# Table checks of a Fourier-plus-experts kernel: four W checks and the row check cut into steps, six compares moved to the score part, no dots in the last block but one

## The chip, the cores and the metric

The kernel runs on one core of a Trainium2 chip. A core has a matrix engine (TensorE, PE in the profile; its weight loads are PEld), a vector engine (VectorE, DVE), a scalar engine (ScalarE, ACT), a general engine (GpSimd, POOL), and SyncE (SP), which here issues most of the DMA transfers. Every engine takes its own instructions in the order written; engines wait for each other through semaphores. The metric is the device time of one execution in microseconds (us). For the kernel before it is 1112.83 us, the median of three runs (1112.5 to 1113.57).

## The reference

With `xn` the layer norm of `x` (2048 tokens, 512 features), the output is `x + A + B`.

```python
# A: real part of a two-dimensional Fourier transform, by given DFT matrices
a = einsum("bsd,ed->bse", xn, dft_hid_re);  b = einsum("bsd,ed->bse", xn, dft_hid_im)
A = einsum("ts,bse->bte", dft_seq_re, a) - einsum("ts,bse->bte", dft_seq_im, b)
# B: 32 heads; each token picks 2 of 64x64 experts per head
q = einsum("nd,dhc->nhc", xn, w_q)
s1 = einsum("nhd,ed->nhe", q[..., :128], k1);  s2 = einsum("nhd,ed->nhe", q[..., 128:], k2)
# top 2 of s1 and of s2, then the top 2 of the 4 sums: top_e (expert), g (softmax weight)
act = gelu(einsum("nd,nhkd->nhk", xn, u[top_e]))
B = einsum("nhk,nhk,nhkd->nd", g, act, v[top_e])
```

The DFT matrices are inputs like any other. The kernel uses their symmetries (it folds rows and columns together and multiplies a quarter of the matrix), so it must also check that the matrices it was given have these symmetries; if one had not, a general path at the end of the program would be taken. The tables are checked by reading their mirrored parts side by side, subtracting (or adding) them, and summing absolute values.

## The kernel before

**Three parts follow each other.** A first part (up to about 70 us) normalises `x` and does the Fourier transform with folded matrices. The score part (72 to 442 us) runs 8 groups of heads times 16 token tiles: 12 matmuls (L799) give a tile's scores, ACT copies them out of PSUM (L804), DVE takes the best of each 64 (L807, L811), and POOL and DVE turn them into expert numbers and gates. Part B (from about 457 us) works on blocks of 128 tokens, 14 of them, numbered 0 to 13. The last two tiles of tokens take another way: their experts' rows are fetched one by one.

**One block of part B.** `u_part(b)` (L959) multiplies the block by all of `u` in 8 steps, called cg here, of 48 matmuls; after each step ACT applies the gelu (L962). The gates are put into a dense matrix by `g_mm(b, tg)` (L996), four times per block: DVE builds two one-hot tables `L` (L983, twice) and `R` (L991, L994), and PE multiplies them into a pair of PSUM banks called `g`. `w_part(b, tg)` then makes weights: DVE multiplies `act` by `g` in place (L1007), ACT rounds to 16 bit (L1012), DVE takes the remainder (L1015). `v_part(b)` (L1024) multiplies by `v` in 8 steps of 12 matmuls, and `finish(b)` (L1039) adds the result to `y` and stores it. The program runs `v_part(b)`, then `u_part(b + 2)`, with `g_mm` and `w_part` of the blocks between them at fixed steps. There are two pairs of `g` banks, so a `g_mm` can start only when the L1015 of the `g_mm` two before it is done. A block has four L1015; the last stands on DVE shortly before the block's `finish`. Blocks 12 and 13 have no `u_part` after them; block 12 is the last but one. The stretch of a block on DVE is counted here from the `finish` of the block before it to its own.

**What runs beside it.** Three streams fill DVE, ACT and POOL. (1) Checks: `compare(n)` for n in 0 to 63 loads 512 KB of the sequence matrices into a buffer of the ring `w` (three buffers, `WB`), DVE subtracts the mirrored parts (L755, L761; other lines where a tile holds row 0), ACT sums absolute values (L781, L783). `compare_w(n)`, n = 64 to 67, does the same with the hidden matrices W, and `compare_r(64)` with rows 0. (2) `fit(n)` has ACT measure largest values of the scaled weights, also in a `w` buffer. (3) The dots of the last two token tiles: POOL fetches a row (L1050), DVE multiplies and sums it (L1066), ACT scales it (L1076 to L1079), POOL adds it (L1084).

**What sets the order.** Each step of `v_part` or `u_part` calls `paced`, which takes the next entries of a list so that the list ends on time, in turn for the fits and for the checks (`units`), and `pick`, which takes dots. `after(k, f)` puts `f` off by k steps, and `hold` ties its instructions behind the step's last matmul in the order of the program; this order is fixed when the program is built, and adds no wait. The compares in `EARLY` are done in the score part instead, at the steps in `at_k`: there POOL subtracts in place of DVE, and the ring `cx` with three buffers is used. `verdict()` sums all checks up in the last block.

Of the kernel before, what the change touches and what calls it, by code (L numbers as in the profile page):

```python
# [15 lines left out]
AF = mybir.ActivationFunctionType  # L16
# [20 lines left out]
def tile_fnet_peer(ctx, tc, x, ca, cb, c5, wt, wf, wr, wq, kt, ut, vn, uv, out):  # L37
# [55 lines left out]
    EARLY = [*range(8, 24), *range(40, 52)]  # L93
# [462 lines left out]
    def part_b(safe, stS, stP, stE, xt, u_sb, cmp_p):  # L556
# [299 lines left out]
        at_k = [7, 10, *(16 * j + i for j in range(1, 7) for i in (0, 4, 7, 9) if (j, i) != (2, 0)), 112, 122, 125]  # L856
# [252 lines left out]
        def compare_r(n):  # L1109
# [14 lines left out]
            def work():  # L1124
                for ri, odd, e in cls:
                    sgn = (((1, 1, 1), (-1, 1, -1)), ((-1, -1, 1), (1, -1, -1)))[ri][odd]
                    f = (-1 if ri else 1) * sgn[1] * sgn[2]
                    m = ALU.add if ri else ALU.subtract
                    nc.vector.tensor_tensor(tv[e, 1], tv[e, 1], tv[e, 0], op=ALU.subtract if sgn[0] > 0 else ALU.add)
                    nc.vector.tensor_tensor(tv[e, 3], tv[e, 3], tv[e, 2], op=ALU.subtract if f > 0 else ALU.add)  # L1130
                    nc.vector.tensor_tensor(t[e, 0::2, 2:4], t[e, 0::2, 2:4], t[e, 0::2, 0:2], op=m)
                    if odd and ri:
                        nc.vector.tensor_copy(t[e, 2, 0:2], t[e, 0, 0:2])
                    elif odd == ri:
                        nc.vector.memset(t[e, 2, 0:2], 0.0)
                after(2, lambda: nc.scalar.activation(tf[:, P:], tf[:, P:], AF.Abs, accum_out=chk[:, n:n + 1]))

            after(2, work)

        def compare_w(n):  # L1140
# [7 lines left out]
            if half:  # L1148
# [4 lines left out]
            nc.vector.tensor_reduce(asum[:, n:n + 1], v[0], axis=AX.X, op=ALU.add, apply_absolute_value=True)  # L1153
            nc.vector.tensor_tensor(v[1][:, even], v[1][:, even], v[0][:, even], op=op)
            nc.vector.tensor_tensor(v[1][:, odd], v[1][:, odd], v[0][:, odd], op=po)
            nc.vector.tensor_tensor(v[3][0:1], v[3][0:1], v[2][0:1], op=op)
            nc.vector.scalar_tensor_tensor(v[3][:, even], v[0][:, even], not0, v[3][:, even],  # L1157
                                           op0=ALU.mult, op1=ALU.subtract)
            nc.vector.scalar_tensor_tensor(v[3][:, odd], v[0][:, odd], not0, v[3][:, odd],  # L1159
                                           op0=ALU.mult, op1=ALU.add)  # L1160

            r = v[2][0:1]
            a, m = (slice(0, P, 2), slice(P, 256, 2)) if ri else (slice(1, P - half, 2), slice(P + 1, 256 - half, 2))
            nc.vector.tensor_tensor(r[:, m], r[:, m], r[:, a], op=op)  # L1164
            nc.vector.memset(r[:, 1 - ri:P:2], 0.0)  # L1165
            if half and not ri:
                nc.vector.memset(r[:, 255:256], 0.0)
            nc.vector.scalar_tensor_tensor(v[2], v[0], not0, v[2], op0=ALU.mult, op1=op)  # L1168
            if ri:
                nc.scalar.activation(v[0][0:1, 0:P], v[0][0:1, 0:P], AF.Abs, accum_out=chk[0:1, 69 + half:70 + half])  # L1170
            c = P - half
            nc.vector.tensor_tensor(v[0][:, P:P + c], v[0][:, P:P + c], v[0][:, 0:c], op=op)  # L1172
            if half and not ri:
                nc.vector.memset(v[0][:, 255:256], 0.0)
# [318 lines left out]
```

## Time and profile before

| What | us |
|---|---|
| median of three runs | 1112.83 |
| the profiled execution | 1110.31 |
| its span, first to last instruction | 1108.5 |
| PE busy | 1070.5 (97%) |
| DVE busy | 963.9 (87%) |
| ACT busy | 717.3 (65%) |
| POOL busy | 595.4 (54%) |

The profiled execution lasted 1.8 us longer than its span, which leaves out what lies around the first and the last instruction. A row of the timeline has the start and the duration in us, the engine, the line, the operation, the output and inputs by the program's names, the shape, how many were merged (x), and in brackets how long the engine sat idle before it and what ended that. A row of the view by windows has, for one stretch, the busy time of each engine with its number of instructions, then the granted clock of the matrix engine (1.00 is full speed), the share of the DMA engines, and GB/s.

### The profile page before, as it was taken

What the parts mean: (1) busy time and instruction counts of PE and PEld (TensorE: products, weight loads), DVE (VectorE), ACT (ScalarE), POOL (GpSimd) and SP (SyncE); (2) the same over time, 40 slices, a digit from 0 to 9 for tenths busy, and PEclk for the clock granted to TensorE, in tenths of its full rate; (3) what the DMA queues carried; (4) which work ended last, traced back from release to release, by engine and by line L of the source; (5) the groups of instructions that cost most, each with busy time, mean ns of one, the idle gap of its engine ahead of it and who ended that gap; (6) DMA issues with size and microseconds to landing.
All of it is one profiled execution on the core that took longest, in us unless ns stands there. A gap on an engine that the chain in (4) does not pass through costs nothing. (4 is left out here: it accounts for less than half of the span.)

```text
span 1108.5 us, 28483 instructions
## 1 busy us (share of the span) xinstructions
PE 1070.5 (97%) x11070; PEld 696.6 (63%) x11070; DVE 963.9 (87%) x2748; ACT 717.3 (65%) x1326; POOL 595.4 (54%) x553
## 2 busy tenths in 40 slices
PE   5899999999999999999989999999999999999987
PEld 4355555454544544987675967858667696776933
DVE  6879897979999999987999798999998889998971
ACT  3566657778788767533756766668666776767650
POOL 0013537588797846211646575665575656556431
PEclk9799999999999999999999999999999999999999
DMA  8248153435445331463568667766876667666511
GB/s 326 84 168 288 39 210 99 174 130 208 152 153 197 110 123 65 152 212 92 183 189 248 193 206 244 223 220 191 242 232 214 209 204 252 222 200 200 166 29 51
DMA packets 84936, 196.78 MB, mean 178 GB/s; under 512 B 10770, under 2 KB 27559, under 8 KB 84792
## 3 DMA queue, kind: packets, MB, share of 16 engines
q1 hardware_dynamic: 63898, 123.55, 33.0%
q0 software_dynamic: 20736, 71.31, 21.7%
q8 instruction: 88, 1.44, 0.5%
q14 instruction: 56, 0.46, 0.1%
q10 hardware_dynamic: 158, 0.01, 0.0%
HBM read 177.74 MB, written 17.10 MB: 176 GB/s over the span
## 5 line engine op out<-in xcount | busy, mean ns | idle before, releaser
L799 PE MATMUL s<-m,xq 128*128 128x512 f16 x1536 | 338.9, 379 | 0.0
L959 PE MATMUL z<-xb,u 128*128 128x128 f16 x5376 | 306.4, 220 | 0.0
L959 PEld LDWEIGHTS <-u 128*128 128x128 f16 x5376 | 302.1, 98 | 0.0
L1024 PE MATMUL v<-v,act 128*128 128x512 f16 x1344 | 300.2, 382 | 1.6 <-DVE act L1015 1.6
L1084 POOL TENSOR_TENSOR ov<-ov,ga 128x512 f32<-128x512 f32 x128 | 176.9, 1382 | 206.9 <-ACT ga L1079 173.4
L799 PEld LDWEIGHTS <-xq 128*128 128x128 f16 x1536 | 148.3, 98 | 171.3 <-issue 0.2
L1024 PEld LDWEIGHTS <-act 128*128 128x128 f16 x1344 | 129.6, 98 | 153.2 <-issue 4.5
L983 DVE TENSOR_TENSOR L<-io_lam,cmp 128x2048 f16<-128x2048 f16 x112 | 154.7, 1405 | 31.2 <-PE g L996 31.1
L1050 POOL DMA_INDIRECT ga<-in_uv_dram,eix x128 | 153.4, 1198 | 48.1 <-POOL ov L1084 36.9
L807 DVE MAX8 vals<-ss 128x8 f32<-128x64 f32 x1024 | 152.5, 216 | 14.0 <-ACT ss L804 14.0
L962 ACT ACTIVATE act<-z,scl 128x512 f32<-128x512 f32 x112 | 76.1, 681 | 93.6 <-PE z L959 92.9
L811 DVE FIND_INDEX8 idx<-vals,ss 128x8 uint16<-128x256 f32 x256 | 107.1, 419 | 0.0
L804 ACT ACTIVATE ss<-s,wsc 128x512 f32<-128x512 f32 x112 | 75.5, 680 | 43.1 <-PE s L799 33.8
L1079 ACT ACTIVATE ga<-ga,za 128x512 f32<-128x512 f32 x128 | 92.3, 722 | 10.2 <-ACT za L1077 0.4
L781 ACT ACTIVATE cx<-cx 128x896 f32<-128x896 f32 x64 | 60.6, 947 | 48.7 <-DVE cx L761 36.3
L1066 DVE SCALAR_TENSOR_TENSOR ga<-ga,px 128x512 f32<-128x512 f32 x128 | 85.7, 676 | 0.2
L1012 ACT ACTIVATE act<-g 128x1024 f16<-128x1024 f32 x56 | 73.2, 1308 | 18.2 <-DVE g L1007 18.2
L1007 DVE SCALAR_TENSOR_TENSOR g<-act,scl,g 128x1024 f32<-128x1024 f32 x56 | 71.6, 1279 | 10.7 <-ACT act L962 6.6
L1015 DVE TENSOR_TENSOR act<-g,act 128x1024 f16<-128x1024 f32 x56 | 72.7, 1298 | 6.6 <-ACT act L1012 6.5
L169 POOL TENSOR_TENSOR wq<-wq,wh 128x1024 f16<-128x1024 f32 x26 | 55.5, 2136 | 24.2 <-ACT wq L166 23.7
L996 PE MATMUL g<-R,L 128*128 128x32 f16 x1792 | 53.8, 176 | 13.0 <-DVE act L1015 12.5
L996 PEld LDWEIGHTS <-L 128*128 128x128 f16 x1792 | 51.6, 96 | 21.7 <-DVE act L1015 8.7
(281 smaller groups left out, 1298.4 us busy)
## 6 DMA issues: line engine op xcount, KB each, us to landing
cx<-in_cb_dram SPq DMA_DIRECT2D x50, 448.0 KB
wq<-in_wq_dram SPq DMA_DIRECT2D x32, 512.0 KB
fit<-in_wq_dram SPq DMA_DIRECT2D x28, 512.0 KB
uv<-in_ut_dram SPq DMA_DIRECT2D x16, 512.0 KB
uv<-in_vn_dram SPq DMA_DIRECT2D x16, 512.0 KB
cx<-in_cb_dram SPq DMA_DIRECT2D x28, 224.0 KB
xq<-in_x_dram SPq DMA_DIRECT2D x8, 512.0 KB
xt_d<-xq SPq DMA_DIRECT2D x16, 256.0 KB
```

The costliest lines, as they stand in the source:

```text
L799: mm = nc.tensor.matmul(ps, xt[i][:, l, kd, :], m[:, r, kd, :], start=(n == 0), stop=(n == 3 * KD - 1))
L807: nc.vector.max(vals[:, i, w, :, h], s[:, g, :])
L811: nc.vector.max_index(idx[:, i, w].rearrange("p k h -> p (k h)"), vals[:, i, w, 0:2].rearrange("p k h -> p (k h)"), s[:, w * HC:g + 1, :]. ...
L959: mm = nc.tensor.matmul(p[:, cc * P:(cc + 1) * P], ug[:, l, c % 2, kd, :], xb[:, r, kd, :], start=(n == 0), stop=(n == 3 * KD - 1))
L962: GL[mm.ins.name] = nc.scalar.activation(act[:, cg * 4:cg * 4 + 4, :].rearrange("p c n -> p (c n)"), p, AF.Gelu_apprx_tanh, scale=zsc)
L983: nc.vector.tensor_tensor(L.rearrange("p t (l two) -> p t l two", two=2), io_lam.rearrange("p (l two) -> p l two", two=2).unsqueeze(1).to_ ...
L996: i = nc.tensor.matmul(p[:, hf, t * NC:(t + 1) * NC], L[:, t, :], R[:, hf * 16 + t, :], start=True, stop=True)
L1024: mm = nc.tensor.matmul(pv, w16[:, c, :, l], vg[:, r, c % 2, :], start=(c == 0 and k == 0), stop=(c == NC - 1 and k == 2))
L1050: nc.gpsimd.indirect_dma_start(out=t, out_offset=None, in_=uv, in_offset=bass.IndirectOffsetOnAxis(ap=eix[:, n].rearrange("p k h -> p (k h ...
L1066: nc.vector.scalar_tensor_tensor(t, t, 1.0, T["x"], op0=ALU.mult, op1=ALU.mult, accum_out=T["z", n][:, s:s + 1])
L1079: nc.scalar.activation(t, t, AF.Copy, scale=z)
L1084: T["a"] = nc.gpsimd.tensor_tensor(o, o, t, op=ALU.add)
```

## The change

Four things change. `EARLY` has 34 compares instead of 28 (38, 39 and 52 to 55 are added), so six more run in the score part (steps 18, 22, 34, 44, 46, 115 and 118 are new in `at_k`, step 23 is gone), and 30 instead of 36 are left for part B. The four `compare_w` go from the end of the list of checks to places 3, 9, 15 and 21 of it, and `compare_r` from place 2 to place 6; by the pacing, the work of the W checks on DVE then falls in the stretches of blocks 2, 4, 6 and 8 and that of the rows in the stretch of block 3, where before W fell in those of blocks 11 and 12 and the rows in that of block 1. `compare_w` no longer does its ten to twelve DVE instructions at once but in four pieces, one each at 2, 3, 4 and 5 steps behind the load, and the sum on ACT at 7; `compare_r` does its four classes at steps 3 to 6 and the sum at 8. The dots picked in block 12 are left out there and picked in block 13. From L857 on, lines of the changed kernel are one higher, and more from L1125 on.

```diff
-    EARLY = [*range(8, 24), *range(40, 52)]
+    EARLY = [*range(8, 24), *range(38, 56)]
...
-        at_k = [7, 10, *(16 * j + i for j in range(1, 7) for i in (0, 4, 7, 9) if (j, i) != (2, 0)), 112, 122, 125]
+        at_k = [7, 10, 16, 18, 20, 22, 25, 34, 36, 39, 41, 44, 46,
+                *(16 * j + i for j in range(3, 7) for i in (0, 4, 7, 9)), 112, 115, 118, 122, 125]
...
         def compare_r(n):
...
-            def work():
-                for ri, odd, e in cls:
...
-                after(2, lambda: nc.scalar.activation(tf[:, P:], tf[:, P:], AF.Abs, accum_out=chk[:, n:n + 1]))
-
-            after(2, work)
+            for k, c in enumerate(cls):
+                after(3 + k, lambda c=c: work(*c))
+            after(8, lambda: nc.scalar.activation(tf[:, P:], tf[:, P:], AF.Abs, accum_out=chk[:, n:n + 1]))
...
         def compare_w(n):
...
-            after(2, lambda: nc.scalar.activation(f, f, AF.Abs, accum_out=chk[:, n + 1:n + 2]))
+            for k, part in enumerate((first, second, third, last)):
+                after(2 + k, part)
+            after(7, lambda: nc.scalar.activation(f, f, AF.Abs, accum_out=chk[:, n + 1:n + 2]))
...
-        units.insert(2, lambda: compare_r(64))
+        for n in range(4):
+            units.insert(3 + 6 * n, units.pop())
+        units.insert(6, lambda: compare_r(64))
...
                 if b and b + 2 != NB:
                     pick(mm, 2 if b + 1 == NB else 1)
-                elif b:
-                    pick(mm, cg % 2)
```

The order of DVE at three places shows what this moves. A row has the line, the operation, the outputs and inputs with buffer numbers, and the shape; `cx_r` is the tile of the row check, `cx` that of a compare or a W check, `ga` a dot, `g` a `w_part`'s product, `act` its remainder.

**The row check.** Before, on DVE in block 1, ahead of the block's last `act`:

```order
L1130 TENSOR_TENSOR cx_r<-cx_r 4x256
L1066 SCALAR_TENSOR_TENSOR ga_9_7478,za_7117<-ga_9_7478,px_7116 128x512
L1131 TENSOR_TENSOR cx_r<-cx_r 4x2x128
L1129 TENSOR_TENSOR cx_r<-cx_r 3x256
L1130 TENSOR_TENSOR cx_r<-cx_r 3x256
L1007 SCALAR_TENSOR_TENSOR g_2_7709<-act_6973,scl,g_2_7709 128x32x32
L1131 TENSOR_TENSOR cx_r<-cx_r 3x2x128
L1129 TENSOR_TENSOR cx_r<-cx_r 4x256
L1130 TENSOR_TENSOR cx_r<-cx_r 4x256
L1015 TENSOR_TENSOR act_6973<-g_1_7583,act_6973 128x32x32
```

After, on DVE in block 3, ahead of the second `act`:

```order
L1129 TENSOR_TENSOR cx_r<-cx_r 3x256
L1130 TENSOR_TENSOR cx_r<-cx_r 3x256
L1067 SCALAR_TENSOR_TENSOR ga_25_8643,za_7165<-ga_25_8643,px_7164 128x512
L1131 TENSOR_TENSOR cx_r<-cx_r 3x2x128
L1135 MEMSET cx_r 3x128
L1129 TENSOR_TENSOR cx_r<-cx_r 4x256
L1130 TENSOR_TENSOR cx_r<-cx_r 4x256
L1067 SCALAR_TENSOR_TENSOR ga_26_8716,za_7165<-ga_26_8716,px_7164 128x512
L1016 TENSOR_TENSOR act_7810<-g_3_8673,act_7810 128x32x32
```

Five of the twelve subtractions now stand ahead of this `act`; the others follow, ahead of the third one.

**The last block but one.** Before, on DVE in block 12, between the first `g` of block 13 and its `act`, with a W check and a dot between them:

```order
L1007 SCALAR_TENSOR_TENSOR g_0_16064<-act_15714,scl,g_0_16064 128x32x32
L1157 SCALAR_TENSOR_TENSOR cx_16377<-cx_16377,not_87 128x128
L1159 SCALAR_TENSOR_TENSOR cx_16377<-cx_16377,not_87 128x128
L1164 TENSOR_TENSOR cx_16377<-cx_16377 1x64
L1007 SCALAR_TENSOR_TENSOR g_1_16340<-act_15714,scl,g_1_16340 128x32x32
L1165 MEMSET cx_16377 1x64
L983 TENSOR_TENSOR L_5792<-io_lam,cmp_15718 128x2048
L1168 SCALAR_TENSOR_TENSOR cx_16377<-cx_16377,not_87 128x256
L1066 SCALAR_TENSOR_TENSOR ga_61_16011,za_11802<-ga_61_16011,px_11801 128x512
L983 TENSOR_TENSOR L_5793<-io_lam,cmp_15718 128x2048
L1172 TENSOR_TENSOR cx_16377<-cx_16377 128x127
L1015 TENSOR_TENSOR act_15714<-g_0_16064,act_15714 128x32x32
```

After, at the same place:

```order
L1008 SCALAR_TENSOR_TENSOR g_0_16078<-act_15737,scl,g_0_16078 128x32x32
L1008 SCALAR_TENSOR_TENSOR g_1_16344<-act_15737,scl,g_1_16344 128x32x32
L984 TENSOR_TENSOR L_5839<-io_lam,cmp_15741 128x2048
L992 TENSOR_TENSOR R_5841<-io_c,cmp_15741 128x1024
L755 TENSOR_TENSOR cx_16381<-cx_16381 128x256
L755 TENSOR_TENSOR cx_16381<-cx_16381 128x512
L995 TENSOR_TENSOR R_5841<-R_5841,cmp_15741 128x1024
L1016 TENSOR_TENSOR act_15737<-g_0_16078,act_15737 128x32x32
```

Six W instructions and a dot are gone from between the two; one `L` has moved ahead, and `R` and a compare have come in. In the order of PE, the `g_mm` that waits for this `act` stands 36 matmuls of `v_part` behind the one before it, where it stood 39 behind it.

**The end of a block.** Before, on DVE at the end of block 9, up to the block's last `act`:

```order
L1007 SCALAR_TENSOR_TENSOR g_2_14070<-act_13340,scl,g_2_14070 128x32x32
L991 TENSOR_TENSOR R_5794<-io_c,cmp_14134 128x1024
L994 TENSOR_TENSOR R_5794<-R_5794,cmp_14134 128x1024
L1066 SCALAR_TENSOR_TENSOR ga_32_13994,za_11802<-ga_32_13994,px_11801 128x512
L1015 TENSOR_TENSOR act_13340<-g_1_13947,act_13340 128x32x32
```

After, at the same place:

```order
L1008 SCALAR_TENSOR_TENSOR g_2_14893<-act_14167,scl,g_2_14893 128x32x32
L1067 SCALAR_TENSOR_TENSOR ga_42_14670,za_11838<-ga_42_14670,px_11837 128x512
L992 TENSOR_TENSOR R_5840<-io_c,cmp_14960 128x1024
L995 TENSOR_TENSOR R_5840<-R_5840,cmp_14960 128x1024
L755 TENSOR_TENSOR cx_14932<-cx_14932 128x512
L755 TENSOR_TENSOR cx_14932<-cx_14932 128x256
L1016 TENSOR_TENSOR act_14167<-g_1_14774,act_14167 128x32x32
```

A compare's two subtractions now stand right ahead of the last `act`. Over blocks 1 to 11, a compare stood there in five blocks before (2, 4, 6, 8 and 10) and stands there in all eleven after.

More of the change, by code (lines that the diff above doesn't have):

```diff
@@ L1168, in compare_w, with first @@
[L1168 to L1174, printed above, removed]
+            r = v[2][0:1]
+            def first():
+                nc.vector.tensor_reduce(asum[:, n:n + 1], v[0], axis=AX.X, op=ALU.add, apply_absolute_value=True)
+                nc.vector.tensor_tensor(v[1][:, even], v[1][:, even], v[0][:, even], op=op)
+                nc.vector.tensor_tensor(v[1][:, odd], v[1][:, odd], v[0][:, odd], op=po)
@@ new lines, in second, with third @@
+            def second():
+                nc.vector.tensor_tensor(v[3][0:1], v[3][0:1], v[2][0:1], op=op)
+                nc.vector.scalar_tensor_tensor(v[3][:, even], v[0][:, even], not0, v[3][:, even],
+                                               op0=ALU.mult, op1=ALU.subtract)
+                nc.vector.scalar_tensor_tensor(v[3][:, odd], v[0][:, odd], not0, v[3][:, odd],
+                                               op0=ALU.mult, op1=ALU.add)
+            def third():
+                a, m = ((slice(0, P, 2), slice(P, 256, 2)) if ri else
+                        (slice(1, P - half, 2), slice(P + 1, 256 - half, 2)))
+                nc.vector.tensor_tensor(r[:, m], r[:, m], r[:, a], op=op)
+                nc.vector.memset(r[:, 1 - ri:P:2], 0.0)
+                if half and not ri:
+                    nc.vector.memset(r[:, 255:256], 0.0)
+                nc.vector.scalar_tensor_tensor(v[2], v[0], not0, v[2], op0=ALU.mult, op1=op)
```

42 lines of the change are left out of this document (19 added, 23 removed).

## The prediction, made before the changed kernel was run

> **What bounds the kernel now.** I read the page's busy shares first, then the view of who waited for whom on PE.
>
> ```profile
> PE 1070.5 (97%) x11070; PEld 696.6 (63%) x11070; DVE 963.9 (87%) x2748; ACT 717.3 (65%) x1326; POOL 595.4 (54%) x553
> PE g L996 <- DVE act L1015: 12.5, 8, 3.9
> PE v L1024 <- DVE act L1015: 1.6, 1, 1.6
> ```
>
> PE is busy 97% of the span, so the time can only fall by what PE idles, or runs at a lower clock. The change adds no matmul and drops none. In part B PE waits for one thing alone: the remainder `act` (L1015) of a `w_part`, 12.5 + 1.6 = 14.1 us in nine waits. PE's timeline places them:
>
> ```profile
> 561.93 0.97 PE L996 MATMUL g<-R,L 128*128 128x32 f16 x32 [3.10 <-DVE act L1015]
> 609.54 0.96 PE L996 MATMUL g<-R,L 128*128 128x32 f16 x32 [0.28 <-DVE act L1015]
> 689.72 0.95 PE L996 MATMUL g<-R,L 128*128 128x32 f16 x32 [0.26 <-DVE act L1015]
> 793.17 0.96 PE L996 MATMUL g<-R,L 128*128 128x32 f16 x32 [0.91 <-DVE act L1015]
> 818.07 0.95 PE L996 MATMUL g<-R,L 128*128 128x32 f16 x32 [1.68 <-DVE act L1015]
> 981.07 0.96 PE L996 MATMUL g<-R,L 128*128 128x32 f16 x32 [2.08 <-DVE act L1015]
> 1050.38 0.95 PE L996 MATMUL g<-R,L 128*128 128x32 f16 x32 [0.28 <-DVE act L1015]
> 1063.68 0.95 PE L996 MATMUL g<-R,L 128*128 128x32 f16 x32 [3.92 <-DVE act L1015]
> ```
>
> The ninth stands in the chain of waits, at 1081.46. A wait costs more than its length where the clock falls behind it, as the view by windows shows for the stretches behind three of them (the share before the DMA's is the granted clock):
>
> ```profile
> 561.90:569.50 7.60, 7.57 (x124) 7.57 (x125) 7.46 (x14) 3.23 (x8) 0.00 (x0) 0.78 0.47 168
> 818.00:826.00 8.00, 7.93 (x58) 3.73 (x58) 7.94 (x13) 6.02 (x14) 4.66 (x5) 0.79 1.03 321
> 1063.60:1071.00 7.40, 7.32 (x55) 3.48 (x55) 6.53 (x9) 3.44 (x5) 2.18 (x2) 0.77 0.25 35
> ```
>
> Lost there: 7.60 x 0.22, 8.00 x 0.21 and 7.40 x 0.23, so 1.7 us each, 5.1 together. Waits and clock make 19.2 us; no more than that can be won in part B.
>
> **The change part by part.** *Rows.* At 562 the row check is what made `act` late:
>
> ```profile
> L1130 DVE TENSOR_TENSOR cx_r<-cx_r x4: 405/414/1485, 551.1 to 560.2; 3x256 f32<-3x256 f32 x2, 4x256 f32<-4x256 f32 x2
> L1131 DVE TENSOR_TENSOR cx_r<-cx_r x4: 405/418/1319, 552.6 to 561.9; 3x256 f32<-3x256 f32 x2, 4x256 f32<-4x256 f32 x2
> ```
>
> Four of each of these, and four like them at L1129, 0.41 us each and two of them drawn out to 1.3 and 1.5, stand almost all in one section: some 7 us. After the change five stand ahead of one `act` and seven behind it, so about 2.1 and 2.9 us, against 2 us for a compare (below), which DVE takes at such places without a wait. I take the 3.10 and its 1.7 of clock as gone: 4.8 us.
>
> *W and the dots in block 12.* Two chains meet at 1063. DVE, from the chain of waits, and ACT, from the timeline:
>
> ```profile
> 1054.83 1.29 DVE g L1007
> 1056.12 1.15 DVE cx L1157
> ...
> 1060.45 0.60 DVE ga L1066 x2
> 1061.06 1.14 DVE L L983
> ...
> 1062.40 1.24 DVE act L1015
> 1048.53 0.31 ACT L1170 ACTIVATE cx<-cx 1x128 f32<-1x128 f32 x1 [3.07 <-DVE cx L1168]
> 1054.13 0.67 ACT L962 ACTIVATE act<-z,scl 128x512 f32<-128x512 f32 x1
> ```
>
> ACT stood 3.07 us before a W sum, so the last gelu came at 1054.13, though PE had ended the block's `u_part` before the `g_mm` of 1050.38; from `g` to the end of `act` DVE then took 8.8 us (1054.83 to 1063.64). After the change ACT has no W sum there, and I take the gelu to come 3 us earlier. From `g` to the end of `act` DVE then has two `g`, an L, R and its product, a compare and `act`: 2 x 1.29 + 1.14 + 2 x 0.69 (a row below) + 2.1 (below) + 1.24 = 8.4 us. So `act` ends 3 + 0.4 = 3.4 us earlier, while PE comes 3 matmuls earlier (20.48 / 94, so 0.22 each, 0.7 in all): 3.92 + 0.7 - 3.4 leaves a wait of 1.2 us. The bounds are none (the compare alone without POOL beside it) and 4.2 (the gelu no earlier); I take 1.2, since the row names the W sum as what ACT waited for. The 0.28 at 1050 goes too, as W stood ahead of that `act`, and with them 1.7 of clock. Won: 3.92 + 0.28 + 1.7 - 1.2 = 4.7 us.
>
> The wait at 1081 stays. The `finish` of block 12 stands ahead of the last `act` in both orders, so DVE cannot start that `act` before the last matmul of block 12:
>
> ```profile
> 1079.46 0.75 DVE y L1039
> 1080.22 1.20 DVE act L1015
> 1081.46 20.48 PE v L1024 x94
> ```
>
> *Where W goes, and the compares.* DVE's load, of all, of the W checks and of the compares:
>
> ```profile
> 490.00:1003.00 513.00, 504.69 (x6730) 377.21 (x6727) 465.14 (x641) 341.36 (x727) 297.84 (x235) 0.99 0.68 207
> 1003.00:1064.00 61.00, 15.91 (x43) 6.29 (x16) 0.00 (x0) 1.00 0.54 162
> 490.00:1003.00 513.00, 75.11 (x118) 46.45 (x140) 0.00 (x0) 0.99 0.68 207
> ```
>
> Four W checks cost DVE 15.9 us, 4.0 each; 36 compares 75.1, so 2.1 each. Into the blocks before 1003 come 15.9 and six compares, 12.5, go: DVE stays as full as it is, 465 of 513 us. ACT gives 6 x 46.45 / 36 = 7.7 us and takes 6.3, and SP loads 2 MB of W in place of 3 MB of compares, so neither queue grows. So the other waits (0.28, 0.26, 0.91, 1.68, 2.08) are not relieved; what counts is where the compares stand. The last wait shows it, on DVE's timeline of the end of block 10:
>
> ```profile
> 974.74 1.97 DVE L991 TENSOR_TENSOR R<-io_c,cmp 128x1024 f16<-128x1024 f16 x1
> 976.74 0.69 DVE L994 TENSOR_TENSOR R<-R,cmp 128x1024 f16<-128x1024 f16 x1
> 977.35 2.47 DVE L755 TENSOR_TENSOR cx<-cx 128x256 f32<-128x256 f32 x2
> 979.75 1.27 DVE L1015 TENSOR_TENSOR act<-g,act 128x1024 f16<-128x1024 f32 x1
> ```
>
> A compare stands ahead of the block's last `act`. This was so in blocks 2, 4, 6, 8 and 10, with waits of 0.28, 0, 0.91, 0 and 2.08 us: 0.65 each, 3.3 in all. After the change it is so in all eleven: 11 x 0.65 = 7.2. In blocks 4, 6 and 8 pieces of a W check stand in the same section, 1 to 2 us of DVE more, part of it in slack: 1.0. The 0.26 and 1.68 I leave at 0.5. So these waits grow from 5.2 to 8.7 us, and of waits as long as 1.5 us, which halved the clock in three of five cases, I expect one or two: 2.5 us of clock against 1.7. Bounds: no wait at all wins 6.9; 2.08 at each block's end costs 11 x 2.08 - 5.2 = 17.7, with 1.7 of clock at every second one 9 more.
>
> The Trainium skill (TensorE: Matmul & The Clock Gate, section "Why this matters for your kernels") warns of idle gaps above about 3 us alone. By that rule no wait that I expect would cost clock, and the sum would be 2.5 us better. The trace disagrees: the wait of 1.68 us was followed by the halved clock, and the measurement decides.
>
> *The score part.* The six compares go to POOL and ACT:
>
> ```profile
> 118.00:457.00 339.00, 0.00 (x0) 28.10 (x54) 62.55 (x78) 1.00 0.40 136
> 160.00:202.00 42.00, 42.00 (x271) 22.81 (x270) 36.13 (x192) 28.16 (x53) 27.66 (x31) 1.00 0.40 134
> L807 DVE MAX8 vals<-ss x1024: 167/216/238, 80.1 to 449.1; 128x8 f32<-128x64 f32 x171
> ```
>
> 27 compares (54 instructions on ACT, two each) took POOL 62.6 us and ACT 28.1, so 2.3 and 1.0 each. Three more fall into 160 to 202, where POOL has 14.3 us free and ACT 13.8, and PE never idles; they need 7 and 3. DVE's MAX8 keeps its 0.2 us whatever POOL does. I take nothing; the bounds are 0 and, if a table for the next group comes late, about 3 us. The dots moved into block 13 run while PE has 20.48 us of `v_part` left and cost nothing there; without that cover they would be three instructions of about 0.75 us, as `y` of the same size above.
>
> **The sum.** 4.8 + 4.7 - (8.7 - 5.2) - (2.5 - 1.7) = 5.2 us. The profiled execution, 1110.31 (span 1108.5 and 1.8 around it), would come to 1105.1. The runs' median, 1112.83, is 2.5 above it; from there the forecast is 1107.6.
>
> **Rivals.** *The ends of blocks go well* (0.17): compares meet no POOL work, the waits at the ends (3.3 of today's 5.2) vanish beside the 9.5 of rows and W, and some 13 us are won: 1100. For it: blocks 4 and 8 had a compare there and no wait. Against it: DVE's 465 of 513.
>
> *No change* (0.17): the waits at the ends and their clock reach about 5.2 + 1.7 + 9.5 = 16.4 us, 1.5 a block, and eat what rows and W give: 1112.8. For it: the section of the last `act` is where DVE is latest today.
>
> *Slower* (0.15): a compare at each block's end, with POOL's sum of dots at the same time,
>
> ```profile
> L1084 POOL TENSOR_TENSOR ov<-ov,ga 128x512 f32<-128x512 f32 x128 | 176.9, 1382 | 206.9 <-ACT ga L1079 173.4
> L991 DVE TENSOR_TENSOR R<-io_c,cmp x56: 666/682/2493, 452.6 to 1063.5; 128x1024 f16<-128x1024 f16 x56
> ```
>
> each of which can draw an R or a subtraction out by about its own 1.4 us, as R's 0.68 to 2.49. If eight ends went like block 10's, 8 x 2.08 - 5.2 = 11.4 more of waits and four times 1.7 of clock, less today's 1.7, against 9.5 won make +7: 1120. It decides from a mean of 1.7 us at a block's end, clock included. The Trainium skill (SBUF — State Buffer, section "SBUF: two separate sides") says that DVE and GpSimd hold a shared pair of ports for whole instructions and the loser is blocked; by that rule this rival would be the common case. The rows agree that it happens, but their median is the undisturbed time.
>
> *The W checks hold `w` buffers longer* (inside the slower one): the sum at step 7 keeps one of three buffers, later loads on SP stand behind it, and DVE waits for a compare's data.
>
> **Numbers.** Forecast 0.51, as the rivals leave it. A measurement of this kernel tells 0.2%, 2.2 us, from no change. Faster: 0.51 and 0.17 give 0.68; same 0.17; slower 0.15. Range: 1099.5, with most of the blocks' ends free, to 1114.5, some 2 us above no change; the forecast's own is 1103 to 1111.
>
> **What would show it.** PE's waits at 562, 1050 and 1063 gone, the one of about 1.6 at block 12's end still there; new waits for L1016 at ends of blocks, 0 to 2 us, below 9 us in all; POOL some 14 us busier in the score part without a PE wait. Wrong if a wait of over 2 us stands ahead of block 13's third `g_mm`, if the blocks' ends sum to more than 12 us, or if PE idles between 118 and 457.

## Result, and the profile after

The changed kernel takes 1115.66 us, the median of 12 executions (1109.96 to 1118.14), beside 1112.10 for 12 of the kernel before on the same chip (1108.93 to 1113.57). The ratio is 1.0035, with an interval of 1.0019 to 1.0051: slower by 0.35%, where 0.5% faster was forecast, and outside the range of 1099.5 to 1114.5. The profiled execution took 1112.97 us with a span of 1111.1, against 1110.31 and 1108.5 before. Of all executions behind this document one, of the version `w_end` below, took 6233 us, for a reason that no trace shows; it counts in that version's median and not in its ratio.

Two lengths tell where that went. The score part, from the first score copy (L804) to the first matmul of block 0's first `g_mm`, grew from 377.2 to 385.1 us. Part B, from there to the end, shrank from 651.9 to 647.2 us. So 7.9 us were lost in the part that the prediction took at nothing, and 4.7 won in the part that it worked out.

**Part B came out as forecast in sum.** The timeline of PE in the changed kernel, with all its waits behind block 0 (lines are one higher than before, L997 is `g_mm`, L1016 the remainder `act`):

```profile
566.12 0.96 PE L997 MATMUL g<-R,L 128*128 128x32 f16 x32 [0.46 <-DVE act L1016]
612.64 0.96 PE L997 MATMUL g<-R,L 128*128 128x32 f16 x32 [0.83 <-DVE act L1016]
648.63 0.95 PE L997 MATMUL g<-R,L 128*128 128x32 f16 x32 [1.61 <-DVE act L1016]
663.12 0.96 PE L997 MATMUL g<-R,L 128*128 128x32 f16 x32 [1.31 <-DVE act L1016]
709.24 0.96 PE L997 MATMUL g<-R,L 128*128 128x32 f16 x32 [0.42 <-DVE act L1016]
827.05 1.01 PE L997 MATMUL g<-R,L 128*128 128x32 f16 x32 [3.02 <-DVE act L1016]
897.43 0.97 PE L997 MATMUL g<-R,L 128*128 128x32 f16 x32 [0.85 <-DVE act L1016]
1023.26 0.95 PE L997 MATMUL g<-R,L 128*128 128x32 f16 x32 [0.39 <-DVE act L1016]
1034.94 0.96 PE L997 MATMUL g<-R,L 128*128 128x32 f16 x32 [0.20 <-DVE act L1016]
1082.36 0.59 PE L1025 MATMUL v<-v,act 128*128 128x512 f16 x2 [0.84 <-DVE y L1040]
1083.55 16.79 PE L1025 MATMUL v<-v,act 128*128 128x512 f16 x77 [0.60 <-DVE act L1016]
```

The waits of 3.10 at 562 and 3.92 at 1063 are gone, new ones of 0.2 to 3 us stand ahead of block 12, and 1.4 us stay at block 12's end. Nine waits of 9.1 us, the 1.4, and the clock behind two of them,

```profile
648.00:657.00 9.00, 8.37 (x62) 4.04 (x62) 8.97 (x11) 6.76 (x14) 6.29 (x6) 0.81 0.63 182
827.00:836.00 9.00, 8.95 (x64) 4.29 (x64) 8.91 (x11) 5.24 (x10) 7.38 (x7) 0.81 0.84 296
```

(9.00 x 0.19 = 1.7 us each, the clock standing ahead of the DMA share) make 13.9 us. The prediction's terms for the same things make 8.7 + 1.2 + 1.6 + 2.5 = 14.0.

**The score part did not.** PE has two waits between 200 us and part B, neither of which was there before:

```profile
239.68 2.75 PE L799 MATMUL s<-m,xq 128*128 128x512 f16 x12 [1.26 <-ACT ss L804]
429.55 8.69 PE L799 MATMUL s<-m,xq 128*128 128x512 f16 x28 [3.80 <-ACT ss L804]
```

Behind the second the clock is halved, as the view by windows has it:

```profile
427.80:434.70 6.90, 5.15 (x13) 1.85 (x13) 6.83 (x53) 6.87 (x11) 2.13 (x1) 0.51 0.35 111
```

The halving begins at 427.80, inside the wait. PE worked in 5.15 of these 6.90 us, at half its speed, so 2.6 us are lost to the clock. With 5.1 us of waits that makes 7.7, about the 7.9 by which the part is longer.

*The first place, step 48.* Here the expert numbers of a finished group are worked out (`routing`, L645 and on), by POOL and DVE in turn. POOL's timeline ahead of it, of the kernel before and of the changed one:

```profile
224.43 2.13 POOL L169 TENSOR_TENSOR wq<-wq,wh 128x1024 f16<-128x1024 f32 x1
226.52 2.13 POOL L608 TENSOR_TENSOR u<-uv,u 128x1024 f16<-128x1024 f32 x1
228.61 1.81 POOL L755 TENSOR_TENSOR cx<-cx 128x768 f32<-128x768 f32 x1
230.49 0.46 POOL L761 TENSOR_TENSOR cx<-cx 128x128 f32<-128x128 f32 x1
230.91 0.32 POOL L645 TENSOR_TENSOR c<-vals 128x64 f32<-128x64 f32 x1
```

```profile
216.27 1.82 POOL L755 TENSOR_TENSOR cx<-cx 128x768 f32<-128x768 f32 x1
...
220.89 0.46 POOL L761 TENSOR_TENSOR cx<-cx 128x128 f32<-128x128 f32 x1
...
225.49 1.97 POOL L755 TENSOR_TENSOR cx<-cx 128x512 f32<-128x512 f32 x2
227.53 0.46 POOL L761 TENSOR_TENSOR cx<-cx 128x128 f32<-128x128 f32 x1
227.95 2.14 POOL L169 TENSOR_TENSOR wq<-wq,wh 128x1024 f16<-128x1024 f32 x1
230.04 2.13 POOL L608 TENSOR_TENSOR u<-uv,u 128x1024 f16<-128x1024 f32 x1
232.12 1.95 POOL L755 TENSOR_TENSOR cx<-cx 128x512 f32<-128x512 f32 x2
234.15 0.46 POOL L761 TENSOR_TENSOR cx<-cx 128x128 f32<-128x128 f32 x1
234.56 0.32 POOL L645 TENSOR_TENSOR c<-vals 128x64 f32<-128x64 f32 x1
```

In neither is POOL idle between these rows. Two compares more stand in the changed queue, that of step 44 (216.27 and 220.89) and that of step 46 (225.49 and 227.53), and the routing starts at 234.56 in place of 230.91. DVE, ACT and the copies behind ACT's gate instruction wait for it, first before and then after:

```profile
231.81 0.23 DVE L648 TENSOR_TENSOR pm<-c,c 128x64 f32<-128x64 f32 x1 [2.72 <-POOL c L647]
233.25 0.26 ACT L653 ACTIVATE c<-c 128x64 f32<-128x64 f32 x1 [2.96 <-POOL c L650]
```

```profile
235.47 0.23 DVE L648 TENSOR_TENSOR pm<-c,c 128x64 f32<-128x64 f32 x1 [6.81 <-POOL c L647]
236.90 0.26 ACT L653 ACTIVATE c<-c 128x64 f32<-128x64 f32 x1 [6.22 <-POOL c L650]
```

DVE does not make the lost 4 us up. The stretch of one later group, by windows, was as full before as it is now (third of the busy times; before, then after):

```profile
275.00:319.00 44.00, 44.00 (x289) 21.48 (x288) 41.24 (x211) 36.07 (x48) 36.14 (x40) 1.00 0.48 166
```

```profile
278.00:322.00 44.00, 44.00 (x288) 21.46 (x287) 41.24 (x210) 36.26 (x48) 36.13 (x40) 1.00 0.50 168
```

DVE is busy for 41.2 of 44 us in both, and it runs 3 us behind the kernel before from there to the last group: its first MAX8 of step 64 starts at 282.86 instead of 279.59, that of step 105 at 395.12 instead of 392.13. Why the 2.8 us of a group in which it is not busy do not make the delay up is not shown.

*The second place, steps 115 to 118.* There DVE does the last group's gates by itself. Its timeline before and after, with POOL's beside it:

```profile
421.78 0.16 DVE L645 TENSOR_TENSOR c<-vals 128x16 f32<-128x16 f32 x1
422.14 0.17 DVE L648 TENSOR_TENSOR pm<-c,c 128x16 f32<-128x16 f32 x1
422.64 0.16 DVE L650 TENSOR_TENSOR c<-c,c 128x16 f32<-128x16 f32 x1
...
425.99 2.14 POOL L608 TENSOR_TENSOR v<-uv,v 128x1024 f16<-128x1024 f32 x1 [6.24 <-ACT uv L607]
```

```profile
423.26 1.89 DVE L645 TENSOR_TENSOR c<-vals 128x16 f32<-128x16 f32 x1
425.89 1.22 DVE L648 TENSOR_TENSOR pm<-c,c 128x16 f32<-128x16 f32 x1
427.42 0.27 DVE L650 TENSOR_TENSOR c<-c,c 128x16 f32<-128x16 f32 x1
...
422.99 2.13 POOL L608 TENSOR_TENSOR v<-uv,v 128x1024 f16<-128x1024 f32 x1
425.07 2.00 POOL L755 TENSOR_TENSOR cx<-cx 128x256 f32<-128x256 f32 x2
...
427.78 0.21 ACT L653 ACTIVATE c<-c 128x16 f32<-128x16 f32 x1 [7.05 <-DVE c L650]
```

Before, POOL stood idle while DVE did this, and from L645 to the end of L650 it took 1.0 us. Now POOL runs a compare, a subtraction and a second compare from 420.50 on, the same small instructions are drawn out from 0.16 to 1.89 and from 0.17 to 1.22 us, and the same stretch takes 4.4 us. ACT waits for them with the score copies behind it in its queue, 7.05 us instead of 5.16, and the 3 us of backlog add to it: PE stands 3.80 us.

### The profile page after: what moved, and what is told of

The parts are those of the page before. It is cut to its first block, busy times and chain, and to the rows that moved or that the text cites. A ratio compares the mean times of both kernels' runs of the same rounds, so it can differ in the third digit from the quotient of the medians.

```text
span 1111.1 us, 28470 instructions
## 1 busy us (share of the span) xinstructions
PE 1069.7 (96%) x11070; PEld 694.6 (63%) x11070; DVE 956.8 (86%) x2732; ACT 715.4 (64%) x1314; POOL 613.7 (55%) x571
## 3 DMA queue, kind: packets, MB, share of 16 engines
q8 instruction: 88, 1.44, 0.5%
## 5 line engine op out<-in xcount | busy, mean ns | idle before, releaser
L1085 POOL TENSOR_TENSOR ov<-ov,ga 128x512 f32<-128x512 f32 x128 | 182.4, 1425 | 203.5 <-ACT ga L1080 166.0
L984 DVE TENSOR_TENSOR L<-io_lam,cmp 128x2048 f16<-128x2048 f16 x112 | 153.7, 1398 | 36.4 <-PE g L997 31.7
L804 ACT ACTIVATE ss<-s,wsc 128x512 f32<-128x512 f32 x112 | 75.6, 681 | 26.0 <-PE s L799 15.3
L1016 DVE TENSOR_TENSOR act<-g,act 128x1024 f16<-128x1024 f32 x56 | 72.5, 1295 | 7.7 <-ACT act L1013 7.6
L755 POOL TENSOR_TENSOR cx<-cx 128x512 f32<-128x512 f32 (+2 forms) x60 | 65.8, 1115 | 4.1 <-DMA cx<-in_cb_dram 4.1
L997 PEld LDWEIGHTS <-L 128*128 128x128 f16 x1792 | 51.2, 96 | 18.8 <-DVE act L1016 8.2
```

The lines of the kernel that those rows point to most:

```text
L984: nc.vector.tensor_tensor(L.rearrange("p t (l two) -> p t l two", two=2), io_lam.rearrange("p (l two) -> p l two", two=2).unsqueeze(1).to_ ...
L1016: nc.vector.tensor_tensor(w16[..., 1], w, w16[..., 0], op=ALU.subtract)
L1085: T["a"] = nc.gpsimd.tensor_tensor(o, o, t, op=ALU.add)
```

## Experiments

"Score part" and "part B" are the two lengths from above, of the profiled execution; the ratio is to the kernel before on the same chip. The medians of the kernel before on those chips were 1112.65 to 1114.72.

| kernel | compares in the score part | score part | part B | median us | ratio (95%) |
|---|---|---|---|---|---|
| before | 28 | 377.2 | 651.9 | 1112.10 | 1 |
| changed | 34 | 385.1 | 647.2 | 1115.66 | 1.0035 (1.0019 to 1.0051) |
| `s_only` | 34 | 384.8 | 655.3 | 1120.13 | 1.0052 (1.0029 to 1.0074) |
| `m46` | 34 | 382.7 | 655.5 | 1116.97 | 1.0030 (1.0013 to 1.0048) |
| `m115` | 34 | 381.1 | 647.9 | 1112.39 | 0.9998 (0.9983 to 1.0012) |
| `mall` | 34 | 378.7 | 647.9 | 1110.14 | 0.9972 (0.9957 to 0.9986) |
| `mall2` | 34 | 384.5 | 649.2 | 1115.15 | 1.0005 (0.9979 to 1.0031) |
| `rows` | 34 | 381.2 | 646.0 | 1110.49 | 0.9969 (0.9949 to 0.9988) |
| `w_end` | 34 | 386.0 | 650.5 | 1116.33 | 1.0001 (0.9978 to 1.0023) |
| `dots` | 34 | 380.9 | 650.6 | 1115.86 | 1.0015 (0.9993 to 1.0037) |
| `mall3` | 34 | 378.0 | 648.7 | 1111.59 | 0.9987 (0.9968 to 1.0006) |
| `mall59` | 34 | 378.0 | 652.3 | 1109.72 | 0.9977 (0.9961 to 0.9994) |
| `rows3` | 34 | 378.2 | 646.9 | 1107.63 | 0.9950 (0.9933 to 0.9967) |
| `b_only` | 28 | 377.5 | 645.1 | 1107.02 | 0.9945 (0.9923 to 0.9967) |
| `b_rows` | 28 | 377.6 | 647.1 | 1107.42 | 0.9958 (0.9940 to 0.9976) |
| `b_wend` | 28 | 377.2 | 650.0 | 1110.70 | 0.9985 (0.9969 to 1.0002) |
| `b_dots` | 28 | 377.4 | 652.8 | 1109.12 | 0.9971 (0.9952 to 0.9990) |

The medians are of 8 to 12 executions. One profiled execution need not be a median one, so the columns of the two parts, from one execution each, are weaker than the ratios.

### The six compares alone, and three of them elsewhere

`s_only` is the kernel before with the `EARLY` and the `at_k` of the change, and nothing else of it.

> The kernel before, with only the six added compares in the score part (28 become 34, at the steps of the change); W, the rows and the dots stay as they were. Theory (the six compares make DVE late at steps 46 to 49 and 115 to 117, and PE waits for ACT's score copies behind that): the first matmul of block 0 in part B starts 7 us later than before, at about 464 us, PE waits for the score copy L804 some 5 us in two places, at about 239 and 429 us; part B has six compares less, 12.5 us of DVE, and wins perhaps 3 to 4 of its 14 us of waits, so the time is about 1115. Rival (the score part does not matter, and part B as changed lost the time): the start of block 0 stays at 456.6 and the time is at or below the kernel before, 1108 to 1112.

The other three are the changed kernel with other steps in `at_k`; the number of compares, the loads and part B stay:

```diff
 at_k, from the first step to 46, and from 112 on
-changed  7, 10, 16, 18, 20, 22, 25, 34, 36, 39, 41, 44, 46            112, 115, 118, 122, 125
+m46      7, 10, 16, 18, 20, 22, 25, 28, 34, 36, 39, 41, 44            112, 115, 118, 122, 125
+m115     7, 10, 13, 16, 18, 20, 22, 25, 30, 34, 36, 39, 41, 44, 46    112, 122, 125
+mall     7, 10, 13, 16, 18, 20, 22, 25, 28, 30, 34, 36, 39, 41, 44    112, 122, 125
```

> The changed kernel, with one compare taken from step 46 to step 28. Theory (46 puts POOL's compare ahead of the routing at 48, DVE stands idle for it and stays 3 us behind until step 112; 115 and 118 do the same again): the wait of 1.26 us at 239 us is gone, that at 429 us falls from 3.8 to about 2.1 us, block 0 starts at 459 to 461 us in place of 463.9, the time is about 1112. Rival A (any compare in the score part costs about the same 1.2 us, wherever it stands): no change of the start, 463.9. Rival B (115 and 118 alone do it): the start falls by the 1.26 us only, to 462.6.

> The changed kernel, with two compares taken from steps 115 and 118 to steps 13 and 30. Theory: the wait of 1.26 us at 239 us stays, the one at 429 us falls from 3.8 to about 1.0 us and the halved clock behind it goes, so block 0 starts at about 458 us, the time is about 1110. Rival A (any compare costs the same wherever it stands): no change of the start, 463.9. Rival B (115 and 118 alone do it): the start is at 457.3 us, with no second wait.

> The changed kernel, with the compares of steps 46, 115 and 118 taken to steps 13, 28 and 30; the number of compares in the score part stays 34. Theory: PE does not wait between 118 us and the start of part B, block 0 starts at 456 us as in the kernel before, part B keeps what it won, and the time is 7.9 us below the changed kernel: about 1108, some 4 us faster than before. Rival A (any compare in the score part costs about 1.2 us): the start stays near 464 and the time near 1115.

`s_only` has the two waits of the changed kernel, 1.27 us at 241 and 3.94 us at 431, and a score part that is 7.6 us longer. Its part B, with six compares less than before, won nothing, where 3 to 4 us had been expected. It was 3.4 us longer in the profile, of which some 2.3 us are short stops of PE at 472 us that the waits put down to "issue" and not to an engine.

Part by part the score part gives back what is moved away: it is 5.5 us over the kernel before in `m46`, 3.9 in `m115`, 1.5 in `mall`. Each gained less than expected: block 0 starts at 462.5, 461.3 and 458.0 us, where 459 to 461, 458 and 456 were expected. The rival by which any compare costs the same wherever it stands is out, since `mall` has all 34. The rival by which 115 and 118 do it alone said 462.6 for the start of `m46`, about what came, but it is out by `m115`, which has no compare at these steps and still waits 1.38 and 1.96 us. In `m46` the second wait was still 3.37 us, not the 2.1 expected: the compare of step 44 still stands ahead of the routing.

### Queue position or load

> As mall, with the compare of step 44 taken away too: the steps 13 and 44 become 12 and 14, still 34 compares. Theory (POOL is one queue and has no gap from step 43 to the routing at 48; every compare that is added there comes off the routing, DVE and then PE): DVE's lag at step 48 falls from 8.95 to the 7.4 us of the kernel before, the wait of 1.0 us at 426 us goes, score part 377.2 us from the first score copy to block 0 (378.7 in mall), time about 1108.6. Rival (34 compares cost something wherever they stand): score part stays at 378.5 or more.

> As mall, with the compares of steps 25, 28, 30 and 44 at steps 24, 26, 28 and 30, so that none stands between 41 and the routing at 48 and none more than in mall between 8 and 16 (in mall2 the one at 14 had its data late and kept POOL idle for 11.2 us ahead of the routing at 17). Theory (a place in POOL's queue behind which no routing waits is free): no wait of PE between 118 us and part B, DVE's lag at step 48 7.5 us as before, score part 377.2 to 377.7 us; time 1.0 to 1.5 us below mall on the same chip, a ratio to before of about 0.996. Rival (34 compares cost something wherever they stand): PE waits of 1 us or more in the score part and a ratio of 0.997 to 1.000.

> As mall, with the compare of step 44 put behind the routing at 48 instead of ahead of it, at step 59, where POOL has a gap of 2.2 us. The load on POOL, ACT and the DMA queues between 200 and 280 us is the same as in mall. Theory (queue position): lag at step 48 falls from 8.95 to 7.5 us, and PE's wait of 1.0 us at 426 us goes or falls below 0.5; score part 377.2 to 377.8 us. Rival (load): the lag at 64 or 112 is as long as in mall and the wait of 1.0 us stays, score part 378.7.

```diff
 at_k, from the first step to 59
-mall     7, 10, 13, 16, 18, 20, 22, 25, 28, 30, 34, 36, 39, 41, 44, 48, 52, 55, 57
+mall2    7, 10, 12, 14, 16, 18, 20, 22, 25, 28, 30, 34, 36, 39, 41, 48, 52, 55, 57
+mall3    7, 10, 13, 16, 18, 20, 22, 24, 26, 28, 30, 34, 36, 39, 41, 48, 52, 55, 57
+mall59   7, 10, 13, 16, 18, 20, 22, 25, 28, 30, 34, 36, 39, 41, 48, 52, 55, 57, 59
```

`mall59` speaks for the position: the same compare stands behind the routing at 48 and not ahead of it. From the score copy of step 48 to DVE's first MAX8 of it, 8.95 us in `mall` become 7.50 (7.37 before), and the wait of 1.0 us at 426 falls to 0.27. Something of the rival stays, since at step 64 the same length is 5.73 us, as in `mall` (5.69), where the kernel before has 5.31.

In `mall3` the wait is gone. Of the 0.8 us that its score part is still over the kernel before, 0.7 are a longer wait for a table (L984) at block 0's start, 1.03 in place of 0.32 us; why it is longer with 34 compares is open. The ratio of `mall3`, 0.9987, is not the 0.996 expected but lies in the range of its rival, 0.997 to 1.000. So the waits follow the position, and the whole time does not come out by it alone.

`mall2` missed, and shows the same queue from another side, on POOL:

```profile
145.93 1.94 POOL L755 TENSOR_TENSOR cx<-cx 128x512 f32<-128x512 f32 x2 [11.19 <-DMA cx<-in_cb_dram]
147.84 0.32 POOL L650 TENSOR_TENSOR c<-c,c 128x64 f32<-128x64 f32 x1
```

Its load stood on SP behind stores that waited; POOL held still for 11.2 us with a routing step behind the compare, and PE waited 4.09 us at 149. The same score part gave 381 to 386 us in the four kernels that have it, so what was laid on it says little. These are the next three, each with one part of the change undone on `mall2`:

> As mall2, with the row check in one piece as in the kernel before (all twelve instructions two steps after its load, its place in the list of checks unchanged). Theory: its 5 to 7 us stand ahead of one remainder again, PE waits some 3 us more there with the clock halved behind it, some 3 to 5 us slower than mall2, about 1112. Rival (the list around it, not its length, made the wait of 562 us in the kernel before): within 1 us of mall2.

> As mall2, with the four W checks in one piece each and at the end of the list as in the kernel before (rows in pieces at the same pace, dots as in the change). Theory: block 12 waits some 3 us again before its third g_mm, 1.7 us of clock behind it, while the blocks before 1003 have 16 us of DVE work less and lose 1 to 2 us less; 2 to 4 us slower than mall2, about 1111. Rival (W in the first blocks holds the w buffers, so that a compare's data comes late, as in the wait of 2.8 to 3.0 us at 823 us, and DVE is fuller there): those waits and their clock go, and it is 2 to 4 us faster than mall2.

> As mall2, with the dots in the last block but one again, as in the kernel before. Theory: three dots of 0.7 us stand on DVE in block 12 once more; W is no longer there, so its waits grow by at most 1 us; within 1.5 us of mall2. Rival (the dots alone made the wait of 3.9 us of the kernel before): 3 to 5 us slower.

Only `rows` stood out, and on the other side of what was expected of it: faster. Of the 6.5 us by which its profile is shorter than that of `mall2`, 3.3 lie in the score part, where the two are the same. `w_end` was expected 2 to 4 us slower, or by its rival faster, and was neither: PE does not wait for block 13's third `g_mm` there, but 1.99 us at 1040.

### Part B by itself

`b_only` is the changed kernel with `EARLY` and `at_k` of the kernel before. `b_rows`, `b_wend` and `b_dots` undo one part of it each; `rows3` is `mall3` with the row check in one piece. In one piece, all four classes are worked on at two steps behind the load and the sum follows two steps later.

For `rows3` and `b_rows`:

```diff
-            for k, c in enumerate(cls):
-                after(3 + k, lambda c=c: work(*c))
+            after(2, work)
```

For `b_wend`, with `compare_w` in one piece:

```diff
-        for n in range(4):
-            units.insert(3 + 6 * n, units.pop())
-        units.insert(6, lambda: compare_r(64))
+        units.insert(5, lambda: compare_r(64))
```

For `b_dots`:

```diff
                     pick(mm, 2 if b + 1 == NB else 1)
+                elif b:
+                    pick(mm, cg % 2)
```

> As mall3, with the row check in one piece as in the kernel before. On mall2 this was faster by 3.1 us of part B in the profile, against my expectation, but the score part of that kernel varied between runs. Theory after that run (the place in the list, not the pieces, did away with the wait of 3.1 us; the pieces only move 1 to 2 us of DVE work from one section to the next): within 1.5 us of mall3. Rival (pieces relieve a remainder): 3 to 5 us slower than mall3.

> The changed kernel with 28 compares in the score part at the steps of the kernel before, so the pieces, the places and the dots alone; part B has 36 compares besides W, 16 us more of DVE work in 513 us than before. Theory: the score part is 377.2 us as before, the waits at 562 and 1063 are gone, DVE's extra work gives back part of it: part B 648 to 651 us against 651.9, time 1 to 4 us below the kernel before. Rival (the fuller DVE gives all of it back): the time of the kernel before, or above.

> b_only with the row check in one piece at the place that it has in the change. Theory after rows and rows3 (the place in the list did away with the wait at 562 us, the pieces do nothing): within 1.5 us of b_only, 1106 to 1109. Rival (the prediction: pieces keep 3 to 5 us of DVE work away from one remainder): 3 to 5 us slower than b_only, 1110 to 1112.

> b_only with the four W checks whole and at the end of the list, as in the kernel before; the row check stays in pieces at its pace, the dots as in the change. Theory (the prediction: W and ACT's W sums are what made block 12 late): PE waits 3 us or more before block 12's third g_mm with a halved clock behind it, the waits before 1003 are shorter by 1 to 2 us; 3 to 5 us slower than b_only, 1110 to 1112. Rival (the dots made block 12 late): within 1.5 us of b_only.

> b_only with the dots in the last block but one, as in the kernel before. Theory (W's place carries the term): the waits of 1.0 and 0.9 us in block 12 grow by 0 to 1.5 us, the time is within 2 us of b_only. Rival (the dots carry it): 3 to 5 us slower, 1110 to 1112.

`b_only` is 0.55% faster than the kernel before, 6 us where 1 to 4 were expected, with 36 compares in part B and 16 us more of DVE work there. So all that the change lost, it lost by the six compares.

The whole row check is as good as the pieces with 28 compares early (0.9958 beside 0.9945, intervals that overlap). With 34 it is better, 1107.63 (`rows3`) beside 1111.59 (`mall3`) on one chip, where both the theory and the rival had something else. In `mall3` the first five pieces stand ahead of a remainder for which PE does not wait. The other seven stand ahead of the next one, with a wait of 1.64 us at 644. The one after that has no piece ahead of it, and PE waits 2.96 us for it at 658, with 1.7 us of clock. Whole, the check stands ahead of one remainder, and the three waits around are 1.20, 0.45 and 0.76 us. That is 3.9 us, about what the medians differ by. What makes the wait at 658 is not shown: it is 1.3 us in five other versions with the pieces, which have the clock halved just ahead of it, and 3.0 in `m46` and `mall`, which like `mall3` have not.

W whole and at the end brings block 12's wait back as it was, in the PE timeline of `b_wend`; in that of `b_only` it is short:

```profile
1049.44 0.95 PE L996 MATMUL g<-R,L 128*128 128x32 f16 x32 [0.27 <-DVE act L1015]
1062.09 0.95 PE L996 MATMUL g<-R,L 128*128 128x32 f16 x32 [3.91 <-DVE act L1015]
```

```profile
1025.72 0.96 PE L996 MATMUL g<-R,L 128*128 128x32 f16 x32 [1.00 <-DVE act L1015]
1058.43 0.95 PE L996 MATMUL g<-R,L 128*128 128x32 f16 x32 [0.93 <-DVE act L1015]
```

The clock was halved behind the 3.91 too. W's place and its pieces together are worth 0.40% by the ratios, 4.4 us, with the two intervals anything from some 1.5 to 7.5; which of the two does it was not tried. This holds with 28 compares early: in `s_only` and `w_end`, where W also stands whole at the end but the list is shorter, the wait of 3.9 us does not come, and one of 2.0 stands at the end of block 11.

`b_dots` has 2.02 and 0.32 us in block 12 where `b_only` has 0.93, and 1.60 at its end for 0.84 and 0.60: the dots are worth about 1.6 us by these rows. Its median is 0.26% above `b_only`'s by the ratios, 2.9 us, but the intervals overlap.

Three of the versions stand out as faster than both kernels: `b_only` (1107.02, ratio 0.9945), `rows3` (1107.63, ratio 0.9950) and `b_rows` (1107.42, ratio 0.9958). `rows3` and `b_rows` both have the row check whole, with 34 and 28 compares early. So compares added to the score part are worth nothing measurable, even at their best places.

## Why the prediction was wrong

**The step that failed** is "I take nothing", with bounds of 0 and about 3 us, for the score part. It measured 7.9 us, and `s_only` alone 7.6. The argument was that POOL has 14.3 us free in the window from 160 to 202, ACT 13.8, and that "DVE's MAX8 keeps its 0.2 us whatever POOL does". Three things were wrong in it.

1. It read a mean over a window where a queue's position counts. POOL has free time in 160 to 202, but ahead of the routing at 48 its rows follow each other without a gap, and DVE, ACT and PE wait for what stands at that queue's end. The row at 230.91 was there to be read before.
2. It looked at the wrong window. It put three of the added compares into 160 to 202; by the traces one more stands there (POOL is busy 28.92 us in it, before 27.66). Of the others one stands before 160, two just ahead of the routing at 48, and two at 420 to 428. Taking those of steps 46, 115 and 118 elsewhere won 6.4 of the 7.9 us.
3. It priced a wait as if it ended there. The 3 us that DVE lost at 48 were still owed at 112 (its first MAX8 of that step starts at 412.45 instead of 409.46), where the next loss came on top. MAX8 indeed kept its time, but not the short instructions beside it on DVE: 0.16 became 1.89 us next to POOL's subtractions.

The rule of the Trainium skill on the shared ports (SBUF — State Buffer, section "SBUF: two separate sides") bears on the last one. It holds for DVE instructions with two inputs in SBUF, beside a GpSimd instruction that reads SBUF, and for DVE modes that use two ports: whichever of the two starts later is blocked for the whole of the other. The trace agrees. L645 and L648 have two inputs and end at 425.15 and 427.11, right behind POOL's instructions that end at 425.12 and 427.07; MAX8 has one input and stays at 0.2 us throughout.

**Rows in pieces, 4.8 us.** At that place the wait went from 3.10 to 0.46 us and its clock went, so the size came, but not by the reason given: the whole check at the new place does as well, or better, so the place in the list suffices. Pieces at the old place were not run. The count of 0.41 us a piece failed too. The seven behind the first `act` took 7.0 us and not 2.9, since three of them were drawn out, to 1.07, 2.05 and 2.16 us, with POOL's sums of dots beside them. In the changed kernel:

```profile
L1130 DVE TENSOR_TENSOR cx_r<-cx_r x4: 405/408/2164, 629.7 to 638.3; 3x256 f32<-3x256 f32 x2, 4x256 f32<-4x256 f32 x2
L1131 DVE TENSOR_TENSOR cx_r<-cx_r x4: 408/744/2052, 630.7 to 641.3; 3x256 f32<-3x256 f32 x2, 4x256 f32<-4x256 f32 x2
```

The `act` behind them is the one for which PE newly waits 1.61 us at 648.63, with 1.7 us of clock, so the pieces gave much of the term back there.

**W and the dots, 4.7 us.** The chain came as told. In the changed kernel the last gelu starts right behind the end of `u_part` at 1058.2, no longer 4 us later, and the third `g_mm` follows without a wait, where the sum left 1.2 us:

```profile
1058.33 0.67 ACT L963 ACTIVATE act<-z,scl 128x512 f32<-128x512 f32 x1
1066.80 0.95 PE L997 MATMUL g<-R,L 128*128 128x32 f16 x32
```

From `g` to the end of `act` DVE took 6.9 us, not 8.4. With 28 compares early W's share is some 4.4 us and the dots' about 1.6. That W's place did it in the changed kernel, with 34 early, is not shown: `s_only` has no such wait either, with W and the dots as before.

**Other waits, 5.2 to 8.7 us.** In the seven waits before 1000 us 8.5 were measured, by luck. The ends of the eleven blocks were to cost 7.2 and cost 4.1, in six waits; single waits of 1.61 and 3.02 away from them make more than half of the 8.5. (The rows shown ahead of the prediction for block 9 after the change are those of block 10 in the trace. In blocks 4, 5 and 9 a dot stands between the compare and the last `act`.)

The wait of 3.02 is the rival in which DVE waits for a compare's data: in the chain of waits the compare's load, issued at 810.49 and 6.31 us on its way, stands ahead of DVE's L755 at 816.89, for which DVE had been idle 5.52 us. That W held the buffer was argued only, and the runs do not bear it out: with W back at the end the wait at this place was 2.89 us in `s_only`, 3.18 in `w_end` and 1.74 in `b_wend`, and with W in the first blocks 1.77 in `b_only`, 2.96 in `b_rows` and 3.23 in `b_dots`. What lengthens it, from 1.68 in the kernel before, stays open.

**Clock, 2.5 us:** 3.4. **Block 12's end, 1.6 us:** 1.44. **The rivals on the slower side** were looked for at the ends of blocks in part B; none had the score part as its place. "Wrong if PE idles between 118 and 457" was the sign that came.

**The six compares taken out of part B** were to keep DVE level there beside W's 16 us. `b_only` kept them in and was no slower in part B (645.1 beside 647.2, one profile each). DVE's total in part B did not set its length there. That it goes by what stands ahead of which remainder is what the single waits suggest.

## What to carry over

Before work is moved to an engine with free time, read that engine's queue at the very place: what follows the moved instruction there, who waits for that, and whether the waiting engine has slack to make a delay up. A mean over a window, and one place for several, hide all three. Cutting a check into pieces need not help: with 34 compares early the whole row check was 0.4% faster than the one in pieces.

## What was not expected of the hardware

The length of a wait doesn't tell whether the clock is halved behind it. In the changed kernel a wait of 1.61 us was followed by 3.41 us at half the clock and one of 1.31 not; the same place gave the halving after 1.64 us in `m115` and not after 1.65 in `mall`; after 2.84 us at 823 in `mall` there was none, and after 3.80 at 429 it lasted 6.83 us. The halving comes in steps of 3.41 us, and the steps lie on one grid through an execution: in the changed kernel it begins at 427.8, 649.7 and 827.1 us, 65 and 52 steps apart.

What goes with it is how much of a wait falls into one step of that grid. Over all seventeen profiles, from 115 to 1095 us, there are 29 steps at full clock in which PE idled 2.0 us or more, and the half clock followed each of them. It followed none with 1.6 us or less, and 10 of 19 in between. The 2.84 us in `mall` lie on both sides of an edge of the grid, 1.60 and 1.24 us. The Trainium skill (TensorE: Matmul & The Clock Gate, section "Why this matters for your kernels") warns of gaps above about 3 us; here gaps half as long sufficed, and some nearly as long did nothing.

The same program varies by some us from one execution to the next: 1109.96 to 1118.14 for the changed kernel. That the grid falls differently against its waits may be part of it; with one trace of each kernel that is not shown. A change of 0.3% shows in ratios over some ten executions, and not in a single profile.
